# Attention and ELU-MLP in one kernel: transposed scores in the first batch, one queue of eight PSUM banks, and a sort key for each step

## The chip, the cores and the metric

The kernel runs on one NeuronCore of a Trainium2 chip. TensorE (PE) does the matmuls, VectorE (DVE), ScalarE (ACT) and GpSimd (POOL) the rest; SyncE (SP) issues the DMAs. The metric is device time in microseconds. The kernel before takes 1371.11 us, the median of three runs (1369.72 to 1373.3).

## The reference

```
q_n = q / sqrt(mean(q*q) + 1e-6) * g_q          (the same for k)
scores = q_n @ k_n.T / 8                        batch 8, heads 12, seq 448, head size 64
attn = exp(scores - max(scores));  attn /= sum(attn) + 1e-9
x = attn @ v, heads side by side                3584 tokens x 768
h = x @ w_in                                    768 x 2048
g = where(h > 0, h, exp(min(h, 0)) - 1)
out = g @ w_out                                 2048 x 768
```

## The kernel before

**Units of work.** Heads go in pairs: 48 pairs `p`, six to a batch. The queries of a pair are cut into seven tiles (`T = 7 p + j`, j = 0 to 6) of 128 rows by 448 keys. A float32 operand is split into a high and a low float16 part, so that scores are three matmuls of 448 columns (`s_mm`, L539). A tile's scores lie in one PSUM bank; DVE takes the row maximum (`s_max`, L546), ACT writes exp(score - max) and the row sum (`s_exp`, L560), POOL adds 1e-9 to the sum (`s_z`, L564), DVE inverts it (`s_rec`, L572).

**From the second batch on**, ACT writes the scaled high part into a float16 buffer (`s_hi`, L605; three such buffers, `p16`), DVE the low part (`s_lo`, L610), which frees the bank, and a transposing DMA on SP's queue (`s_tr`, L621) puts the tile into `ptall` with keys on the partitions. There is one such place for a pair, so a pair's transposes wait until the pair before has been multiplied with v: `attend`, L638, 22 matmuls, two at a time on two halves of the array. `x_high` and `x_low` (L645, L657) read that result.

**In the first batch** the weights are still being prepared, and the transposing is done by TensorE: POOL makes a diagonal matrix with the inverse sums (`s_diag`, L576), four float32 matmuls per tile transpose and scale (`s_pe`, L584), ACT copies the result to SBUF (`s_hi`, L601), and `attend` multiplies in float32.

**The MLP** of a batch is 576 matmuls of 448 columns: 288 for the first product (`mlp`, L733; 16 blocks `f` of 18) and 288 for the second (L747; six blocks of 48). It runs beside the attention of the following batch. Each first-product block leaves its bank in five steps (`m1_out`): exp on ACT (L670), a second ACT step (L674), the minimum and maximum on DVE (L678, frees the bank), the high part on ACT (L684), the low part on DVE (L687). A second-product block needs one ACT copy (L708). Below, a pair beside the first product is called an **M1 pair**, one beside the second an **M2 pair**: three and three to a batch.

**Weights.** `conv` splits each of 16 blocks of `w_in` and 24 of `w_out`: ACT L235 and L236, DVE L241 and L265, sums over partitions by `column_sums` (13 or 9 matmuls of 64 columns, L135), then L281/L284 or L306 to L321. Queries and keys are normalised by `qk_square` to `qk_transpose` (L363 to L430).

**Order.** Nothing is scheduled at run time; each engine takes its instructions in the order in which they are written. Time is a counter `h`, 14 units to a pair. The table `SCHED` gives each step an `h` in halves; a loop over `h` writes the steps due, then the MLP matmuls due by a rate (576 for 84 units), in two or three stretches around the score matmuls. For all pairs after the first batch a tile's steps have the same offsets (`tile`, second row), two units apart from tile to tile. Scores are issued for four tiles and then, eight units later, for three; `attend` of the pair before is written right behind those three. The bank queue is first in, first out: five banks, seven from the second batch on; `av` is a bank of its own.

Of the kernel before, what the change touches and what calls it, by code (L numbers as in the profile page):

```python
# [20 lines left out]
NPAIR = H // 2  # L21
# [11 lines left out]
def tile_attention_then_elu_mlp(ctx: ExitStack, tc: tile.TileContext, qk, v, v_scan, gg, w_in, w_out, out):  # L33
# [46 lines left out]
    nc.vector.memset(eps, 1e-6)  # L80

    def cols(t, n):
# [22 lines left out]
        t[:CK].rearrange("p (c q) -> p c q", c=4)  # L105
# [25 lines left out]
    def column_sums(parts, bank):  # L131


        for i, a in enumerate(parts + [tiny]):
            nc.tensor.matmul(bank[:, S:], ones, a, start=i == 0, stop=i == len(parts))  # L135

    def largest(bank, e):
        nc.vector.tensor_reduce(out=e, in_=bank[:, S:], axis=AX.X, op=ALU.max)
        return e
# [74 lines left out]
    def conv(src, i, width, acol, bank, parts):  # L216
# [7 lines left out]
        ws = None  # L224
# [21 lines left out]
        def s_sums():  # L246
            column_sums([upper(t[:, a : a + 64]) for a in range(0, width, 64)], bank)
# [22 lines left out]
        steps = [load, s_act, s_join, s_sign, on_pe(s_sums), s_scale]  # L270
        for fn in parts:
            step = lambda fn=fn: fn(w, ws)
            steps.append(on_pe(step) if fn in late else step)
        loads.add(load)
        return steps

    def conv_in(f):
# [5 lines left out]
        def s_low(w, ws):  # L283
# [6 lines left out]
            w_in, f, WI_W, a_in[:, f : f + 1], sb[4 - f] if f < 2 else av,  # L290
            [s_high, s_low],
        )

    def conv_out(i):
# [30 lines left out]
        def s_store(w, ws):  # L325
# [3 lines left out]
            w_out, i, WO_W, most[:, i : i + 1], mb[i % 2] if i < WO_OWN else av,  # L329
# [129 lines left out]
    def v_steps(b):  # L459

        m1 = dg = None
# [6 lines left out]
        def two():  # L468
            nonlocal dg
# [3 lines left out]
        def three():  # L473
            column_sums([upper(dg[:, :64]), upper(dg[:, 64:])], av)
# [544 lines left out]
```

## Time and profile before

| | |
|---|---|
| median of three runs | 1371.11 us |
| the profiled execution | 1372.15 us, span 1370.3 us |
| mean granted TensorE clock | 0.975 |
| busy in the span: PE, ACT, DVE, POOL | 91%, 64%, 61%, 36% |
| `attend` of pairs 5, 11, 47 starts at | 143.1, 321.2, 1254.6 us |

The span lies 1.85 us below the time of its own execution. Busy time counts recorded instructions, and neighbouring records on one engine overlap slightly, so that the step from start to start is a little shorter than a record. `[3.33 <-PE av L638]` behind a row means that the engine stood idle for 3.33 us and that this instruction ended the wait.

### The profile page before, as it was taken

The page shows a single profiled execution, that of the slowest core. Times are in us where ns is not written, and L with a number is a line of the kernel's source. Part 1 is how long each engine was busy: PE and PEld are TensorE (multiplying, and loading weights), DVE is VectorE, ACT ScalarE, POOL GpSimd, SP SyncE. Part 2 cuts the span into 40 slices and gives each one's busy share as a digit, 9 for nine tenths or more (in the row PEclk, how much of TensorE's full clock was granted, in tenths as well). Part 3 has the DMA queues.
Part 4 walks back from the last instruction along what each step waited for, and adds up shares of the span by engine and source line. Part 5 has one row for each costly group of instructions (what it writes and reads, how often), then busy time and mean ns, then how long its engine had stood idle before and what let it go on. Part 6 is the DMA issues. An engine that isn't in the chain of part 4 may idle for free.

```text
span 1370.3 us, 22209 instructions
## 1 busy us (share of the span) xinstructions
PE 1249.1 (91%) x7564; PEld 724.8 (53%) x7564; DVE 840.8 (61%) x1898; ACT 883.2 (64%) x1857; POOL 488.8 (36%) x823
## 2 busy tenths in 40 slices
PE   4898988989899988999889998999889988999998
PEld 2555444654446643565436644565446644466566
DVE  8998877776665656656665656655666556642310
ACT  7999787656676567756765567746766566743520
POOL 4677543444233422433323432333333333231000
PEclk9999899999999999999999999999999999999999
DMA  9557776886558866597556866588446965574011
GB/s 341 159 171 169 158 179 149 196 199 128 111 120 183 190 108 133 112 209 160 107 117 160 202 124 133 109 199 174 106 105 157 210 121 113 109 151 121 1 44 58
DMA packets 405713, 198.62 MB, mean 145 GB/s; under 512 B 367968, under 2 KB 381920, under 8 KB 405600
## 3 DMA queue, kind: packets, MB, share of 16 engines
q1 hardware_dynamic: 405600, 197.21, 63.6%
q8 instruction: 59, 0.97, 0.3%
q14 instruction: 54, 0.44, 0.1%
HBM read 93.52 MB, written 14.16 MB: 79 GB/s over the span
## 4 chain that ended last, share of the span: by engine, by line
PE 59%; ACT 16%; DVE 11%; DMA 7%; issue 6%; POOL 1%; SPq 0%; ACTq 0%; POOLq 0%; DVEq 0%
PE s L747 22%; PE s L733 10%; PE av L638 7%; PE m L747 6%; DMA ptall<-p 6%; PE s L539 5%; PE m L733 4%; ACT p L605 4%; DVE p L610 3%; ACT s L560 2%; PE m L539 2%; ACT gall L684 2%; DVE st L546 2%; PE s L584 2%; DVE e L678 2%
## 5 line engine op out<-in xcount | busy, mean ns | idle before, releaser
L747 PE MATMUL s<-gall,whos 128*128 128x448 f16 x1184 | 325.0, 354 | 0.1
L610 DVE SCALAR_TENSOR_TENSOR p<-s,st,p 128x448 f16<-128x448 f32 x204 | 139.5, 684 | 256.4 <-ACT p L605 255.0
L733 PE MATMUL s<-x,whi 128*128 128x448 f16 x1022 | 290.0, 364 | 4.3 <-DVE p L610 2.4
L564 POOL TENSOR_SCALAR st<-st 128x1 f32<-128x1 f32 x336 | 78.1, 232 | 589.0 <-ACT s L560 391.8
L747 PEld LDWEIGHTS <-whos 128*128 128x128 f16 x1536 | 221.2, 144 | 80.4 <-issue 13.8
L733 PEld LDWEIGHTS <-whi 128*128 128x128 f16 x1536 | 153.7, 100 | 160.9 <-issue 33.5
L747 PE MATMUL s<-gall,wls 128*128 128x448 f16 x592 | 209.8, 354 | 0.0
L539 PE MATMUL s<-qkt 64*128 64x448 f16 (+1 forms) x840 | 148.5, 369 | 52.6 <-DVE p L610 33.3
L560 ACT ACTIVATE s<-s,st 128x448 f32<-128x448 f32 x204 | 122.7, 602 | 109.5 <-DVE st L546 104.0
L733 PE MATMUL s<-x,wli 128*128 128x448 f16 x511 | 185.7, 363 | 0.0
L605 ACT ACTIVATE p<-s,st 128x448 f16<-128x448 f32 x204 | 127.9, 627 | 60.1 <-DMA ptall<-p 59.0
L546 DVE TENSOR_REDUCE st<-s 128x1 f32<-128x448 f32 x246 | 151.4, 615 | 9.8 <-PE s L539 8.3
L539 PEld LDWEIGHTS <-qkt 64*128 64x128 f16 (+1 forms) x1152 | 55.4, 98 | 173.2 <-issue 141.8
L747 PEld LDWEIGHTS <-wls 128*128 128x128 f16 x768 | 111.3, 145 | 40.3 <-issue 7.7
L610 DVE SCALAR_TENSOR_TENSOR p<-m,st,p 128x448 f16<-128x448 f32 x90 | 61.5, 683 | 112.0 <-ACT p L605 111.5
L392 POOL TENSOR_TENSOR nat<-nat,r 128x896 f32<-128x896 f32 (+1 forms) x48 | 84.7, 1766 | 109.9 <-DVE r L382 108.7
L684 ACT ACTIVATE gall<-e,gsc 128x448 f16<-128x448 f32 x128 | 85.1, 665 | 59.3 <-DVE e L678 59.1
L733 PEld LDWEIGHTS <-wli 128*128 128x128 f16 x768 | 76.8, 100 | 79.2 <-issue 17.0
L687 DVE SCALAR_TENSOR_TENSOR gall<-e,gsc,gall 128x448 f16<-128x448 f32 x128 | 98.2, 767 | 23.3 <-ACT gall L684 22.6
L733 PE MATMUL m<-x,whi 128*128 128x448 f16 x354 | 99.7, 361 | 1.9 <-DVE p L610 1.9
L747 PE MATMUL m<-gall,whos 128*128 128x448 f16 x352 | 98.8, 361 | 1.8 <-DVE p L610 1.8
L674 ACT ACTIVATE e<-e,nisc,isc 128x448 f32<-128x448 f32 x128 | 96.6, 754 | 1.2
(129 smaller groups left out, 1992.0 us busy)
## 6 DMA issues: line engine op xcount, KB each, us to landing
wls<-wl_d SPq DMA_DIRECT2D x48, 512.0 KB, 4.0
nat<-in_qk SPq DMA_DIRECT2D x48, 448.0 KB, 3.9
raws<-in_w_out SPq DMA_DIRECT2D x24, 512.0 KB, 4.7
out<-y SPq DMA_DIRECT2D x48, 224.0 KB, 2.6
vn<-in_v SPq DMA_DIRECT2D x38, 256.0 KB, 3.3
vscan<-in_v_scan SPq DMA_DIRECT2D x36, 224.0 KB, 3.7
whos<-in_w_in SPq DMA_DIRECT2D x10, 768.0 KB, 6.7
ptall<-p SPq DMA_TRANSPOSE x336, 3.1
```

What stands on the lines that cost most here:

```text
L392: nc.gpsimd.tensor_tensor(out=n[:, a:], in0=n[:, a:], in1=r[:, a:], op=ALU.mult)
L539: nc.tensor.matmul(ps[r0 : r0 + n, :S], qq[rows, a, q0 : q0 + n], qq[rows, z, S:], start=(a + z == 0), stop=(a == 1),)
L546: nc.vector.tensor_reduce(out=st[:, 0:1], in_=pss[T][:, :S], axis=AX.X, op=ALU.max, negate=True)
L560: nc.scalar.activation(e, ps, AF.Exp, bias=st[:, 0:1], accum_out=st[:, 1:2])
L605: nc.scalar.activation(p16[:, :S], pss[T][:, :S], AF.Copy, scale=stats[T][:, 2:3])
L610: nc.vector.scalar_tensor_tensor(out=p16[:, S:], in0=ps[:, :S], scalar=r, in1=p16[:, :S], op0=ALU.mult, op1=ALU.subtract)
L638: nc.tensor.matmul(av[64 * h : 64 * h + 64, :S], vs[:, h], ps[h], start=(k == 0), stop=(k == len(terms) - 1),)
L674: nc.scalar.activation(e, e, AF.Identity, scale=isc, bias=nisc)
L684: nc.scalar.activation(g[:, 0], e, AF.Copy, scale=gsc)
L687: nc.vector.scalar_tensor_tensor(out=g[:, 1], in0=e, scalar=gsc, in1=g[:, 0], op0=ALU.mult, op1=ALU.subtract)
L733: nc.tensor.matmul(ph[:, :S], w[:, c, :], x[:, r, :], start=(c == 0 and i == 0), stop=last)
L747: nc.tensor.matmul(py[:, :S], w, g[:, r, :], start=(f == 0 and i == 0), stop=last)
```

## The change

**First batch.** Scores are computed twice. The first time (`s_mm`, two tiles at a time) they serve only for the maximum: `s_max` writes the negated maxima of all seven tiles into one small array and gives the bank back. POOL splits the maxima into two bfloat16 parts (`m_last`, `m_split`). The second time (`t_mm`) they are computed with keys on the partitions, in seven banks per pair; `t_shift` adds the negated maxima to the same banks, with 64 matmuls a pair of 128 columns (or 64), the maxima broadcast as weights and an identity as the moving operand. `t_exp` is then one ACT instruction per tile straight into the buffer that `attend` reads. The sums over keys are eight float32 matmuls with ones (`t_sum`); the inverse is exp(-ln z) on ACT with one Newton step on DVE (`z_log`, `z_inv`, `z_newton`, `x_times`, `x_step`), applied to the result of `attend`. `s_diag`, `s_pe`, and the first batch's `s_exp`, `s_z`, `s_rec` and `s_hi` are gone.

**Banks.** All eight are in one queue; `attend`, `column_sums` and the score tiles take from it.

**Order.** Every step has its own key with three decimals; a heap takes the steps in the order of their keys. The MLP is placed matmul by matmul, with a pace for the first two batches and the old rate afterwards; the offsets of `m1_out` and `m2_out` are a table (`evict`). Pairs from 12 on share one pattern of keys, repeated every 14 units.

```diff
+    banks = [psum.tile([128, S], F32, name=f"b{i}") for i in range(8)]
...
     def s_max(T):
+        p, j = divmod(T, NJ)
+        if by_pe(T):
+            to = mneg[p % 2][:, 8:] if j == NJ - 1 else mneg[p % 2][:, j % 2 * 4 + j // 2 :][:, :1]
+        else:
+            st = stats[T] = small("st", 3, bufs=6)
+            to = st[:, 0:1]
+        nc.vector.tensor_reduce(out=to, in_=pss[T], axis=AX.X, op=ALU.max, negate=True)
+        if by_pe(T):
+            give(pss.pop(T))
...
+    def t_mm(p, c):
+        qq = qkt[p].rearrange("p t j n -> p t (j n)")
+        k0 = S + 128 * c
+        if c < 3:
+            pst[p, c] = [take(), take()]
+        else:
+            ps = take()
+            pst[p, c] = [ps[:64], ps[64:], ps]
+        for a, z in ((0, 0), (0, 1), (1, 0)):
+            for h in (0, 1):
+                rows = slice(64 * h, 64 * h + 64)
+                nc.tensor.matmul(
+                    pst[p, c][h], qq[rows, a, k0 : min(k0 + 128, 2 * S)], qq[rows, z, :S],
+                    start=(a + z == 0), stop=False,
+                )
+
+    def t_shift(p, c):
+        m = mhl[p % 2].rearrange("p t (h i) -> p t h i", h=2)
+        for i in range(4):
+            for t in (0, 1):
+                for h, ps in enumerate(pst[p, c][:2]):
+                    nc.tensor.matmul(
+                        ps[:, 128 * i : min(128 * i + 128, S)],
+                        m[:, t, h, i : i + 1].broadcast_to([128, ps.shape[0]]),
+                        eye if i < 3 else eye2, start=False, stop=(i == 3 and t == 1),
+                    )
+
+    def t_exp(p, j):
+        c, h = divmod(j, 2)
+        ps = pst[p, c][h] if c < 3 else pst[p, c][2]
+        nc.scalar.activation(pt_f32[p % 2][:, j], ps, AF.Exp)
+        give(ps)
...
+        av = avs[p] = take()
...
+    def next_mm(i, key):
+        r = next(moe, None)
+        if r:
+            for d, fn in zip(SCHED["evict"][2 * (i >= 576) + (len(r) == 3)], r, strict=True):
+                at(key + d, fn)
+        if i + 1 < 576 * B:
+            key = pace(i + 1)
+            at(key, next_mm, i + 1, key)
...
-        [-0.5, 0.5, 1.5, 1.5, 2.5, 3, 6, 8.5, 4.5],
+        [169.723, 170.697, 171.11, 172.729, 173.518, 173.963, 177.243],
```

The three places below lie in the fourth batch, beside the first product of the third, where the pattern of the later batches is in force.

TensorE at `attend` of pair 18 and the last three score tiles of pair 19; `vt` is the v of the pair, `qkt` its queries and keys, `s4`, `b3` and the like are banks. Before:

```order
L539 MATMUL s4_71<-qkt_5136 128x448
L539 LDWEIGHTS qkt_5136
L539 MATMUL s2_69<-qkt_5136 128x448
...
L539 MATMUL s3_70<-qkt_5136 64x448
L638 LDWEIGHTS vt_5478
L638 MATMUL av_72<-ptall_135,vt_5478 64x448
...
L733 LDWEIGHTS wli5_114
L733 MATMUL m0_73<-x3_129,wli5_114 128x448
```

And now:

```order
L788 LDWEIGHTS whi5_114
L788 MATMUL b1_68<-x3_145,whi5_114 128x448
...
L689 LDWEIGHTS vt_5660
L689 MATMUL b3_70<-ptall_151,vt_5660 64x448
...
L533 LDWEIGHTS qkt_5373
L533 MATMUL b7_74<-qkt_5373 128x448
L533 LDWEIGHTS qkt_5373
L533 MATMUL b5_72<-qkt_5373 128x448
```

`attend` stood behind three score tiles, each of which waits for a free bank; it now stands ahead of them and takes one bank itself.

ScalarE between `x_high` of pairs 18 and 19 (L560 is `s_exp`, L605 `s_hi`, L670, L674 and L684 the steps of `m1_out`, L401 and L411 copies of keys and queries). Before:

```order
L560 ACTIVATE s4_71,st_5589<-s4_71,st_5589 128x448
L605 ACTIVATE p16_5611<-m1_74,st_5523 128x448
L674 ACTIVATE e_5602<-e_5602,nisc_2177,isc_2176 128x448
L401 ACTIVATE t16_5632<-nat_5316 128x384
L670 ACTIVATE e_5635<-m0_73,sc_2175 128x448
L560 ACTIVATE s2_69,st_5626<-s2_69,st_5626 128x448
L605 ACTIVATE p16_5645<-s4_71,st_5589 128x448
L411 ACTIVATE t16_5632<-nat_5316 128x512
L684 ACTIVATE gall_134<-e_5602,gsc_2178 128x448
L674 ACTIVATE e_5635<-e_5635,nisc_2177,isc_2176 128x448
L560 ACTIVATE s3_70,st_5665<-s3_70,st_5665 128x448
L605 ACTIVATE p16_5680<-s2_69,st_5626 128x448
```

And now (L639 is `s_exp`, L655 `s_hi`, L725, L729 and L739 the steps of `m1_out`, L398 the copy of the keys):

```order
L739 ACTIVATE gall_150<-e_5790,gsc_3591 128x448
L639 ACTIVATE b4_71,st_5802<-b4_71,st_5802 128x448
L655 ACTIVATE p16_5831<-b0_67,st_5664 128x448
L725 ACTIVATE e_5835<-b1_68,sc_3588 128x448
L729 ACTIVATE e_5835<-e_5835,nisc_3590,isc_3589 128x448
L739 ACTIVATE gall_150<-e_5835,gsc_3591 128x448
L725 ACTIVATE e_5864<-b3_70,sc_3588 128x448
L398 ACTIVATE t16_5867<-nat_5420 128x384
L729 ACTIVATE e_5864<-e_5864,nisc_3590,isc_3589 128x448
L655 ACTIVATE p16_5872<-b7_74,st_5776 128x448
L655 ACTIVATE p16_5881<-b5_72,st_5769 128x448
L655 ACTIVATE p16_5891<-b4_71,st_5802 128x448
```

An `s_exp` and the `s_hi` of the tile before it stood next to each other all through the pair; now the exponentials and the high parts come in groups, with whole MLP evictions between them.

VectorE in the same stretch (L610 is `s_lo`, L546 `s_max`, L572 `s_rec`, L678 and L687 steps of `m1_out`, L367 a sum for the next pair). Before:

```order
L610 SCALAR_TENSOR_TENSOR p16_5645<-s4_71,st_5589,p16_5645 128x448
L546 TENSOR_REDUCE st_5665<-s3_70 128x1
L572 RECIPROCAL st_5626<-st_5626 128x1
L687 SCALAR_TENSOR_TENSOR gall_134<-e_5602,gsc_2178,gall_134 128x448
L678 SCALAR_TENSOR_TENSOR e_5635<-e_5635,m0_73 128x448
L610 SCALAR_TENSOR_TENSOR p16_5680<-s2_69,st_5626,p16_5680 128x448
L546 TENSOR_REDUCE st_5709<-s1_68 128x1
```

And now (L651 is `s_rec`, L660 `s_lo`, L733 and L742 steps of `m1_out`, L545 `s_max`, L364 the sum):

```order
L660 SCALAR_TENSOR_TENSOR p16_5872<-b7_74,st_5776,p16_5872 128x448
L733 SCALAR_TENSOR_TENSOR e_5864<-e_5864,b3_70 128x448
L660 SCALAR_TENSOR_TENSOR p16_5881<-b5_72,st_5769,p16_5881 128x448
L742 SCALAR_TENSOR_TENSOR gall_150<-e_5835,gsc_3591,gall_150 128x448
L660 SCALAR_TENSOR_TENSOR p16_5891<-b4_71,st_5802,p16_5891 128x448
L545 TENSOR_REDUCE st_5918<-b7_74 128x1
L545 TENSOR_REDUCE st_5922<-b3_70 128x1
L364 TENSOR_REDUCE ss_5929<-qkt_5911 128x14
L545 TENSOR_REDUCE st_5937<-b0_67 128x1
```

Each maximum stood right behind the `s_lo` of an earlier tile; now the maxima stand together, ahead of or behind a group of `s_lo`.

## Rows read from the trace of the kernel before

**Rows 1.** The page: span, busy time of the engines, and the granted clock in 40 slices of the span, in tenths.
```profile
span 1370.3 us, 22209 instructions
PE 1249.1 (91%) x7564; PEld 724.8 (53%) x7564; DVE 840.8 (61%) x1898; ACT 883.2 (64%) x1857; POOL 488.8 (36%) x823
PEclk9999899999999999999999999999999999999999
```
**Rows 2.** Busy time by stretch: the first batch up to `attend` of pair 5, the second up to that of pair 11, the next six, and what is left after the last `attend`. Columns: stretch, length, busy time of PE, PEld (weight loads), DVE, ACT and POOL with instructions, granted clock, DMA share, GB/s.
```profile
0.00:143.50 143.50, 112.66 (x874) 70.10 (x876) 128.40 (x298) 126.81 (x257) 91.22 (x132) 0.98 0.70 213
143.50:321.16 177.66, 155.99 (x987) 87.27 (x985) 131.62 (x297) 127.67 (x267) 81.92 (x119) 0.94 0.76 170
321.16:1254.62 933.46, 868.37 (x5107) 496.24 (x5109) 559.36 (x1271) 592.11 (x1278) 314.34 (x567) 0.98 0.67 142
1254.62:1370.30 115.68, 112.07 (x603) 71.21 (x602) 21.45 (x34) 36.65 (x56) 1.34 (x5) 1.00 0.13 42
```
**Rows 3.** The same view of the six stretches of three M1 pairs, from one `attend` to the third after it: the first and the second of them and the sum of the six.
```profile
321.16:405.79 84.63, 75.07 (x430) 35.64 (x432) 52.88 (x115) 59.37 (x124) 26.30 (x45) 0.96 0.56 116
475.71:563.26 87.55, 75.56 (x432) 35.65 (x433) 53.59 (x116) 60.42 (x128) 26.64 (x46) 0.96 0.58 114
...
sum 516.60, PE 451.90 PEld 214.16 DVE 321.19 ACT 361.09 POOL 159.47; mean PE 75.32 PEld 35.69 DVE 53.53 ACT 60.18 POOL 26.58
```
**Rows 4.** The same view of the first stretch of three M2 pairs, and of one M1 pair alone.
```profile
405.79:475.71 69.92, 69.91 (x428) 47.16 (x430) 41.81 (x101) 39.61 (x90) 26.96 (x50) 1.00 0.82 182
506.41:534.64 28.23, 24.25 (x145) 11.66 (x146) 16.90 (x38) 19.64 (x41) 8.55 (x15) 1.00 0.51 109
```
**Rows 5.** Waits over the whole span: who waited for whom, total us, times, longest.
```profile
PE s L539 <- DVE p L610: 33.3, 25, 2.7
DVE p L610 <- ACT p L605: 366.5, 259, 4.7
ACT p L605 <- DMA ptall<-p: 87.3, 55, 4.3
```
**Rows 6.** Groups of instructions in the three M1 pairs from 475.71 to 563.26 us: busy time, mean ns of one, idle time before them and what ended it.
```profile
L610 DVE SCALAR_TENSOR_TENSOR p<-s,st,p 128x448 f16<-128x448 f32 x16 | 10.9, 684 | 21.7 <-ACT p L605 21.4
L610 DVE SCALAR_TENSOR_TENSOR p<-m,st,p 128x448 f16<-128x448 f32 x5 | 3.4, 684 | 8.9 <-ACT p L605 8.9
L684 ACT ACTIVATE gall<-e,gsc 128x448 f16<-128x448 f32 x14 | 9.3, 666 | 8.7 <-DVE e L678 8.7
L687 DVE SCALAR_TENSOR_TENSOR gall<-e,gsc,gall 128x448 f16<-128x448 f32 x13 | 10.4, 799 | 0.1
```
**Rows 7.** The timeline of one M1 pair (start us, duration us, what, wait before it), ACT, DVE and SP's queue.
```profile
511.71 0.63 ACT L605 ACTIVATE p<-m,st 128x448 f16<-128x448 f32 x1 [0.81 <-DMA ptall<-p]
512.25 0.75 ACT L674 ACTIVATE e<-e,nisc,isc 128x448 f32<-128x448 f32 x1
512.38 0.68 DVE L610 SCALAR_TENSOR_TENSOR p<-m,st,p 128x448 f16<-128x448 f32 x1 [2.52 <-ACT p L605]
512.90 0.51 ACT L401 ACTIVATE t<-nat 128x384 f16<-128x384 f32 x1
512.98 0.67 DVE L687 SCALAR_TENSOR_TENSOR gall<-e,gsc,gall 128x448 f16<-128x448 f32 x1
513.57 0.62 DVE L546 TENSOR_REDUCE st<-s 128x1 f32<-128x448 f32 x1
514.23 0.61 ACT L560 ACTIVATE s<-s,st 128x448 f32<-128x448 f32 x1 [0.29 <-DVE st L546]
514.85 0.63 ACT L605 ACTIVATE p<-s,st 128x448 f16<-128x448 f32 x1
...
516.22 1.23 SPq L621 DMA_TRANSPOSE ptall<-p  x1
```
**Rows 8.** The first batch: TensorE's timeline, matmuls merged.
```profile
84.07 0.74 PE L539 MATMUL s<-qkt 64*128 64x448 f16 x3
84.74 1.13 PE L584 MATMUL s<-dgz,ex 128*112 128x128 f32 x8
85.70 0.52 PE L135 MATMUL av<-wts,ones 128*128 128x64 bf16 x12
86.06 0.19 PE L135 MATMUL av<-tiny,ones 128*128 128x64 bf16 x1
87.91 3.23 PE L638 MATMUL av<-ptall,gall 112*64 112x448 f32 x16
93.18 0.76 PE L539 MATMUL s<-qkt 64*64 64x448 f16 x6
```
**Rows 9.** Groups of the first 250 us: what the change takes out of the first batch, and `x_low`, whose form the new DVE steps have.
```profile
L560 ACT ACTIVATE ex<-s,st 128x448 f32<-128x448 f32 x42 | 26.5, 632 | 4.1 <-DVE st L572 1.2 <-PE s L584 1.1 <-PE av L135 0.8
L560 ACT ACTIVATION_READ_ACCUMULATOR ex<-s,st 128x1 f32 x42 | 8.5, 202 | 0.0
L601 ACT ACTIVATE ptall<-s 112x512 f32<-112x512 f32 x21 | 12.6, 601 | 0.0
L576 POOL TENSOR_SCALAR dgz<-ident,st 128x128 f32<-128x128 f32 x42 | 23.0, 547 | 7.2 <-DVE st L572 2.0 <-DVE most L138 1.5 <-PE s L584 0.4
L572 DVE RECIPROCAL st<-st 128x1 f32<-128x1 f32 x69 | 10.5, 153 | 1.2 <-POOL st L564 1.2
L652 DVE SCALAR_TENSOR_TENSOR x<-av,vs,x 128x448 f16<-128x448 f32 x6 | 4.0, 671 | 0.0
```

More of the change, by code (lines that the diff above doesn't have):

```diff
@@ L129, in upper, with column_sums @@
         return t.bitcast(BF16).rearrange("p (n w) -> p n w", w=2)[:, :, 1]
-    def column_sums(parts, bank):
-        for i, a in enumerate(parts + [tiny]):
-            nc.tensor.matmul(bank[:, S:], ones, a, start=i == 0, stop=i == len(parts))
+    def column_sums(pairs):
+        bank = take()
+        pairs = pairs + [(ones, tiny)]
+        for i, (w, a) in enumerate(pairs):
+            nc.tensor.matmul(bank[:, :64], w, a, start=i == 0, stop=i == len(pairs) - 1)
+        return bank
     def largest(bank, e):
-        nc.vector.tensor_reduce(out=e, in_=bank[:, S:], axis=AX.X, op=ALU.max)
+        nc.vector.tensor_reduce(out=e, in_=bank[:, :64], axis=AX.X, op=ALU.max)
+        give(bank)
         return e
@@ L246, in s_sums @@
         def s_sums():
-            column_sums([upper(t[:, a : a + 64]) for a in range(0, width, 64)], bank)
+            nonlocal bank
+            bank = column_sums([(ones, upper(t[:, a : a + 64])) for a in range(0, width, 64)])
         def s_scale():
@@ L268, in s_sign @@
             )
[L270 to L275, printed above, removed]
+        steps = [load, s_act, s_join, s_sign, s_sums, s_scale]
+        return steps + [lambda fn=fn: fn(w, ws) for fn in parts]
     def conv_in(f):
@@ L459, in v_steps @@
     def v_steps(b):
-        m1 = dg = None
+        m1 = bank = None
         def one():
@@ new lines, in tile_attention_then_elu_mlp, with t_sum, z_log @@
+    avs, zbs, zes, zas = {}, {}, {}, {}
+    def t_sum(p):
+        zb = zbs[p] = take()
+        pt = pt_f32[p % 2]
+        for c in range(4):
+            for h in (0, 1):
+                nc.tensor.matmul(
+                    zb[64 * h : 64 * h + 64], one3[:, 0 if c < 3 else 1 + h], pt[:, min(2 * c + h, 6)],
+                    start=c == 0, stop=c == 3,
+                )
+    def z_log(p):
+        zes[p] = pool.tile([128, S], F32, tag="e", name="ze", bufs=3)
+        nc.scalar.activation(zes[p], zbs[p], AF.Ln, bias=small9)
@@ new lines, in z_inv, with z_newton, x_times, x_step @@
+    def z_inv(p):
+        nc.scalar.activation(zes[p], zes[p], AF.Exp, scale=-1.0)
+    def z_newton(p):
+        zas[p] = pool.tile([128, S], F32, tag="e", name="za", bufs=3)
+        zb = zbs.pop(p)
+        nc.vector.scalar_tensor_tensor(
+            out=zas[p], in0=zb, scalar=1e-9, in1=zes[p], op0=ALU.add, op1=ALU.mult
+        )
+        give(zb)
+    def x_times(p):
+        av = avs.pop(p)
+        nc.vector.tensor_tensor(out=zes[p], in0=av, in1=zes[p], op=ALU.mult)
+        give(av)
+    def x_step(p):
+        nc.vector.scalar_tensor_tensor(
+            out=zas[p], in0=zas[p], scalar=2.0, in1=zes.pop(p), op0=ALU.subtract, op1=ALU.mult
+        )
```

380 lines of the change are left out of this document (189 added, 191 removed), and 118 rows, old and new, of the table SCHED.

## The prediction

> **What bounds the kernel now.** I read the page first, then busy time by stretch, then the waits, then one pair's timeline. The page says that PE is busy for 91% of the span [rows 1], so most of the time is TensorE's own work; what the change can win is PE's idle time, and where that lies the stretches tell [rows 2]: 30.8 us of 143.5 in the first batch, 21.7 us in the second, 65.1 us in the six that follow, 3.6 us at the end. After the last `attend` both kernels have the same 580 MLP matmuls left, so what counts is when that `attend` comes.
>
> In the six later batches the two kinds of pair differ. Three M2 pairs take 69.92 us with PE busy for 69.91, which is 23.3 us a pair and TensorE alone [rows 4]. Three M1 pairs take 516.6 / 6 = 86.1 us, 28.7 us a pair, though PE issues the same number of matmuls, while ACT is busy for 20.1 us of it and DVE for 17.8 [rows 3]. So no engine is full: 5.4 us a pair are lost to waiting, 18 pairs, 97 us. The clock explains little: one M1 pair at a granted clock of 1.00, the 2.4 GHz level, still takes 28.2 us [rows 4].
>
> The waits give the reason. PE waits for banks that DVE's L610 has not yet freed, 33.3 us under one set of bank names alone; DVE's L610 waits for ACT's L605, 366.5 us in 259 waits; ACT's L605 waits for transposing DMAs to free a float16 buffer, 87.3 us [rows 5]. In three M1 pairs DVE stands 30.3 us in front of L610, 1.4 us for each of 21 tiles, and ACT stands 8.7 us in front of L684 because the DVE step before it is queued behind that L610 [rows 6]. The timeline shows the circle: high part at 511.71, low part at 512.38, an MLP step, the next maximum at 513.57, its exponential at 514.23, the next high part at 514.85 [rows 7]. That is 3.1 us a tile, seven times 22 us, in which ACT and DVE hand over to one another four times a tile; what else ACT has to wait for in a pair (the transposing, `x_high`) comes on top.
>
> **The change part by part, M1 pairs.** The work of each engine in these pairs stays as it was: same steps, same sizes. Order and banks change. `attend` moves ahead of three score tiles, so it waits for one bank instead of three, and the transposing that follows it starts earlier. Exponentials and high parts come in groups of one to three tiles, and no maximum stands any more directly behind a low part that waits for ACT. I followed ACT and DVE by hand through one M1 pair in the new order, with start-to-start steps from the timeline (0.62 us for an exponential, 0.54 for a high part, 0.65 for the MLP's second step) [rows 7]. ACT then has these waits left: 0.7 us for the end of `attend`, 1.0 us for the first maximum behind it, 0.6 and 0.4 us for MLP steps behind maxima on DVE, 0.3 us for the transposing. That is 3.0 us on 20.1 us of work, 23.1 us, about what PE needs by itself. The walk is too smooth in two places. DVE's L687 takes 0.80 us on average where the walk has 0.67 [rows 6, 7], 0.7 us for 5.3 blocks. And it lets every transposing land at its usual time, though the longest wait for one is 4.3 us [rows 5]; I add 1.0 us. That makes 25.0 us a pair. The bounds are 23.3 us, PE alone, and 28.7 us, as before; I take a value nearer to the lower one because the circle that sets 28.7 is taken apart, but not PE's own value, because ACT has hardly more room than the waits listed. 18 pairs at 28.7 - 25.0 = 3.7 us: **67 us less**. The M2 pairs are PE's own work: 0.
>
> Behind `attend`, now earlier, TensorE's queue holds the score tiles; in front of SP's transposes stand the same loads as before. In the second pattern the last three high parts stand together on ACT, and each waits for a buffer that an earlier tile's transposing frees; SP needs 1.23 us to issue one [rows 7]. Queued behind them are the next block's MLP steps, for whose bank PE waits.
>
> **First batch.** Per pair, ACT loses seven exponentials with their read of the sum (0.63 + 0.20 us recorded) and seven copies of 0.60, and gains seven exponentials without a sum and two more passes of that size, nine at 0.63: 10.0 - 5.7, 4.3 us less [rows 9]. DVE loses seven reciprocals of 0.15 us and gains three steps of the form of `x_low`, 0.67 each: 1.0 us more [rows 9]; without the overlap of short records it is nearer to 1.3, 8 us for six pairs with the constants. POOL loses seven diagonal matrices of 0.55 us and the scaling of the sums, 23.0 us and more in the batch [rows 9], against four small copies and subtractions a pair.
>
> TensorE: one tile's scores alone take 0.67 us from start to start, two half-height ones side by side no longer (0.76 recorded), and a tile's transposing 0.96 to 1.1 us [rows 8]: 7 x (0.67 + 1.05) = 12.0 us go. Scores of two tiles side by side, twice, are eight times 0.67 = 5.4 us; `t_sum` has the form of the first batch's `attend`, 3.2 us [rows 8]; `t_shift` has no row. Twelve matmuls of 64 columns start within 0.36 us, 0.03 each [rows 8], and matmuls of 448 columns every 0.22, three to a tile's 0.67; between them 128 columns come to 0.06, 64 of them to 3.8 us a pair. Bounds: 0.03 and 0.22 each, 1.9 to 14 us. I take the value between the two, since the form differs only in the number of columns. Sum 12.4 us against 12.0: nothing. The Trainium skill (TensorE: Matmul & The Clock Gate, Back-to-back issue gap) puts a stream of weight load and 128-column matmul at about 81 ns a matmul; by that `t_shift` would be an estimated 5.2 us a pair, and no run here shows it. It would add 1.4 us a pair to PE, which has 30.8 us free in this batch [rows 2], so the sum below would stay.
>
> DVE and ACT are both nearly full in the first batch, 128.4 and 126.8 of 143.5 us [rows 2]. Relief on ACT and POOL therefore wins little while DVE gets 8 us more; part of that fits into its 15 us of idle time. And one wait is new: no exponential of a pair can run before all its seven maxima. I take **4 us more**, between -5 (ACT's relief closes a third of DVE's idle time) and +12 (8 plus a chain that shows in part).
>
> **Second batch.** Six pairs take 177.7 us, 29.6 each, with PE busy for 156.0 [rows 2]; the same handing over is at work, beside the weights' conversion. Bounds 0 and 21.7 us less; I take **10 us less**, under half, since DVE and ACT still do the conversion.
>
> **Sum.** 1372.15, the profiled execution, + 4 - 10 - 67 = 1299 us. That execution lies 1 us above the median of the three, which puts the median of the changed kernel at 1298; I say 1299.
>
> **Rivals.**
> *A. TensorE becomes the bound of M1 pairs as of M2 pairs.* For it: ACT's 20.1 and DVE's 17.8 us fit into 23.3 [rows 3, 4]. Against it: the waits in the walk. 97 us in the M1 pairs, 22 in the second batch, 5 in the first: 1371 - 124 = 1247 us.
> *B. The waits only change places.* ACT and DVE still cross for each MLP block and each tile; if the groups make one long wait of several short ones, M1 pairs come to 27.5 us. 18 x 1.2 = 22 us less, 4 more in the first batch: 1353 us. If the new keys make no difference in effect to what waits for what, no change is left.
> *C. Slower: the last high parts of a pair wait for transposes.* Three of them stand together on ACT, and MLP steps and their banks behind them. For it: 87.3 us already go in 55 such waits, up to 4.3 us [rows 5]. Against it: `attend` is earlier, and the third needs only the fourth tile's transposing. It decides from 5.4 us of waiting a pair, at which an M1 pair is back at 28.7. At 6 us a pair takes 29.3: 18 x 0.6 = 11 more, 4 in the second batch's pairs, 8 in the first: 1371 + 23 = 1394 us.
>
> **How the numbers follow.** Forecast 0.43, with a range of its own from 1275 to 1330; A 0.20; B 0.21, a quarter of it within 0.3% of before; C 0.16. About 0.3% is what a measurement of this kernel can tell from no change, 1367 to 1375 us. Faster 0.43 + 0.20 + 0.16 = 0.79, same 0.05, slower 0.16. From 1252 to 1376 us: A's lower part (0.08) and C's upper one (0.12) are left out.
>
> **What would show it.** Right: three M1 pairs between two `attend`s at 73 to 78 us; DVE's idle time before the low part under 12 us in three M1 pairs, where it was 30.3; `attend` of pair 5 at 140 to 155 us; about 0.06 us for a matmul of `t_shift`. Wrong: M1 pairs above 27 us with ACT idle before the high parts on transposes (C) or before exponentials on maxima (B); M1 pairs at 23.3 us with PE never idle (A); a first batch beyond 155 us, where the chain from the seventh maximum to the first exponential is longer than I allow.

## The result, and the profile after

The changed kernel takes 1273.31 us (median of 4 runs, 1269.55 to 1274.1) against 1370.49 us for the kernel before on the same chip: 0.928 of it, 95% interval 0.926 to 0.931, or 97 us less. The forecast was 1299 us, 26 us too slow. The measured time lies inside the stated bounds of 1252 to 1376 us, but outside the range of 1275 to 1330 that the forecast had for itself; it is as far from rival A's 1247 us as from the 1299.

The page after: span, busy time of the engines, granted clock in 40 slices, and the chain that ended last.

```profile
span 1271.1 us, 22591 instructions
PE 1215.2 (96%) x7852; PEld 704.2 (55%) x7852; DVE 863.7 (68%) x1883; ACT 860.1 (68%) x1777; POOL 481.1 (38%) x763
PEclk9889899999999999999999999999999999999999
PE 68%; DVE 4%; ACT 2%; issue 1%; POOL 0%; DMA 0%; ACTq 0%; POOLq 0%
```

TensorE is busy for 96% of the span where it was 91% [rows 1]. Busy time by the same four stretches as in [rows 2] (columns as there):

```profile
0.00:151.07 151.07, 116.01 (x1148) 57.35 (x1148) 142.04 (x273) 102.02 (x176) 61.73 (x71) 0.92 0.63 190
151.07:318.85 167.78, 152.40 (x1010) 87.15 (x1009) 139.53 (x298) 128.79 (x269) 87.05 (x119) 0.99 0.83 186
318.85:1155.42 836.57, 834.78 (x5100) 488.33 (x5100) 561.82 (x1279) 591.33 (x1278) 331.04 (x569) 1.00 0.78 160
1155.42:1271.10 115.68, 112.07 (x602) 71.32 (x602) 20.33 (x34) 37.97 (x56) 1.33 (x5) 1.00 0.13 42
```

Against [rows 2] the first batch is 7.6 us longer, the second 9.9 shorter, the six that follow 96.9 shorter, the tail the same: 99.2 us together, the difference of the two spans. In the third stretch PE stands idle for 1.8 us of 836.6, where it stood for 65.1 of 933.5.

The stretches of three M1 pairs, the second and third of six and the sum, as in [rows 3]:

```profile
457.25:527.13 69.88, 69.83 (x426) 34.50 (x426) 52.76 (x118) 57.57 (x119) 27.47 (x43) 1.00 0.77 144
596.90:667.01 70.11, 70.05 (x430) 34.34 (x429) 52.89 (x118) 57.90 (x119) 27.46 (x43) 1.00 0.70 140
...
sum 418.93, PE 417.14 PEld 204.85 DVE 319.62 ACT 347.90 POOL 166.68; mean PE 69.52 PEld 34.14 DVE 53.27 ACT 57.98 POOL 27.78
```

418.93 us instead of 516.60: 97.7 us, so all of the third stretch's gain lies in the 18 M1 pairs, now at 23.3 us like the M2 pairs [rows 4]. Two numbers make it up. PE's idle time falls from 516.60 - 451.90 = 64.7 us to 1.8. And its busy time falls by 34.8 us, from 451.90 to 417.14, for the same work. The granted clock goes from 0.96 [rows 3] (0.96 in the other four stretches too) to 1.00: 0.04 of 516.60 us, some 21 of the 34.8, are matmuls that no longer run at the 1.2 GHz level. What the other 14 are is taken up below the table of runs.

The waits after, those that answer to [rows 5]:

```profile
DVE p L660 <- ACT p L655: 122.6, 101, 4.0
ACT p L655 <- DMA ptall<-p: 66.6, 50, 3.6
PE b L533 <- DVE p L660: 2.4, 3, 1.1
```

The low part's wait for the high part is a third of what it was, PE's wait for the low part's bank is nearly gone, and ACT's wait for the transposing has only shrunk by a quarter. In one stretch of three M1 pairs (457.25 to 527.13 us), the groups that answer to [rows 6]:

```profile
L660 DVE SCALAR_TENSOR_TENSOR p<-b,st,p 128x448 f16<-128x448 f32 x19 | 12.7, 675 | 4.8 <-ACT p L655 4.8
L655 ACT ACTIVATE p<-b,st 128x448 f16<-128x448 f32 x20 | 12.1, 625 | 2.9 <-DMA ptall<-p 1.4 <-DVE st L651 1.1 <-DVE p L660 0.3
L742 DVE SCALAR_TENSOR_TENSOR gall<-e,gsc,gall 128x448 f16<-128x448 f32 x13 | 11.6, 891 | 0.0
L739 ACT ACTIVATE gall<-e,gsc 128x448 f16<-128x448 f32 x14 | 9.3, 665 | 5.3 <-DVE e L733 4.3 <-DVE gsc L493 0.8
```

DVE stands 4.8 us in front of the low parts where it stood 30.6 [rows 6]. ACT still waits 5.3 us in front of the MLP's fourth step, and nothing comes of it: that time now lies beside PE's.

### The profile page after: what moved, and what is told of

It is laid out like the page before. It is cut to its first block, busy times and chain, and to the rows that moved or that the text cites. A ratio compares the mean times of both kernels' runs of the same rounds, so it can differ in the third digit from the quotient of the medians.

```text
span 1271.1 us, 22591 instructions
## 1 busy us (share of the span) xinstructions
PE 1215.2 (96%) x7852; PEld 704.2 (55%) x7852; DVE 863.7 (68%) x1883; ACT 860.1 (68%) x1777; POOL 481.1 (38%) x763
## 4 chain that ended last, share of the span: by engine, by line
PE 68%; DVE 4%; ACT 2%; issue 1%; POOL 0%; DMA 0%; ACTq 0%; POOLq 0%
PE b L802 30%; PE b L788 25%; PE b L533 7%; PE b L689 6%; DVE gall L742 1%; DVE st L545 1%; ACT p L655 1%; DVE p L660 1%; ACT b L639 1%; ACT e L725 0%; DVE e L733 0%; DMA ptall<-p 0%; ACT e L729 0%; ACT gall L739 0%; DVE ss L375 0%
## 5 line engine op out<-in xcount | busy, mean ns | idle before, releaser
L802 PE MATMUL b<-gall,whos 128*128 128x448 f16 x1536 | 417.3, 353 | 2.5 <-DVE gall L742 2.5
L788 PE MATMUL b<-x,whi 128*128 128x448 f16 x1376 | 376.8, 354 | 1.9 <-DVE e L733 1.1
L660 DVE SCALAR_TENSOR_TENSOR p<-b,st,p 128x448 f16<-128x448 f32 x294 | 196.6, 676 | 124.9 <-ACT p L655 122.6
L802 PE MATMUL b<-gall,wls 128*128 128x448 f16 x768 | 272.8, 355 | 0.0
L788 PE MATMUL b<-x,wli 128*128 128x448 f16 x688 | 243.7, 354 | 0.0
L655 ACT ACTIVATE p<-b,st 128x448 f16<-128x448 f32 x294 | 179.8, 628 | 94.2 <-DMA ptall<-p 66.6
L545 DVE TENSOR_REDUCE st<-b 128x1 f32<-128x448 f32 x294 | 173.0, 615 | 89.6 <-PE b L533 89.5
L639 ACT ACTIVATE b<-b,st 128x448 f32<-128x448 f32 x294 | 177.2, 603 | 41.4 <-DVE st L545 38.5
L533 PE MATMUL b<-qkt 64*128 64x448 f16 (+1 forms) x1152 | 142.9, 359 | 14.6 <-DVE mneg L545 8.9
L733 DVE SCALAR_TENSOR_TENSOR e<-e,b 128x448 f32<-128x448 f32 x128 | 79.0, 617 | 92.0 <-ACT e L729 91.7
L739 ACT ACTIVATE gall<-e,gsc 128x448 f16<-128x448 f32 x128 | 85.2, 666 | 45.2 <-DVE e L733 38.9
L742 DVE SCALAR_TENSOR_TENSOR gall<-e,gsc,gall 128x448 f16<-128x448 f32 x128 | 109.2, 853 | 0.2
L689 PE MATMUL b<-ptall,vt 128*64 128x448 f16 x924 | 96.5, 355 | 3.1 <-POOL vt L452 2.9
L729 ACT ACTIVATE e<-e,nisc,isc 128x448 f32<-128x448 f32 x128 | 97.2, 760 | 2.2
L389 POOL TENSOR_TENSOR nat<-nat,r 128x896 f32<-128x896 f32 (+1 forms) x48 | 82.3, 1715 | 39.6 <-DVE r L379 23.3
```

The lines of the kernel that those rows point to most:

```text
L389: nc.gpsimd.tensor_tensor(out=n[:, a:], in0=n[:, a:], in1=r[:, a:], op=ALU.mult)
L533: nc.tensor.matmul(ps[r0 : r0 + n], qq[rows, a, q0 : q0 + n], qq[rows, z, S:], start=(a + z == 0), stop=(a == 1),)
L545: nc.vector.tensor_reduce(out=to, in_=pss[T], axis=AX.X, op=ALU.max, negate=True)
L639: nc.scalar.activation(ps, ps, AF.Exp, bias=st[:, 0:1], accum_out=st[:, 1:2])
L655: nc.scalar.activation(p16[:, :S], pss[T], AF.Copy, scale=stats[T][:, 2:3])
L660: nc.vector.scalar_tensor_tensor(out=p16[:, S:], in0=ps, scalar=r, in1=p16[:, :S], op0=ALU.mult, op1=ALU.subtract)
```

## The experiments

Each kernel is timed against the kernel before on the same chip (medians of before: 1372.4 to 1373.9 us beside the experiments). The measure below is the stretch from `attend` of pair 17 to that of pair 47 beside the whole time: thirty pairs, in which PE alone needs some 697 us. Each trace gives it. A trace is one execution: it lies within 1.7 us of the median in the table, but the one of "before, both" took 1331.96 us, 7 more than its median.

| kernel | time, us | pairs 17 to 47, us | PE busy in them, us |
|---|---|---|---|
| before | 1370.5 | 778.9 | 723.4 |
| before, `attend` early | 1339.6 | 753.5 | 717.4 |
| before, eight banks | 1356.9 | 762.6 | 714.6 |
| before, both | 1325.1 | 744.8 | 713.6 |
| both, and MLP steps closer | 1319.9 | 736.5 | 709.1 |
| both, and earlier tile first | 1310.0 | 729.9 | 710.9 |
| changed | 1273.3 | 698.1 | 697.8 |
| changed, `attend` late | 1289.7 | 712.2 | 698.9 |
| changed, old tiles, `attend` late | 1318.3 | 721.9 | 704.4 |
| changed, old tiles, `attend` early | 1286.4 | 696.2 | 695.2 |
| the same, MLP on the old grid | 1288.1 | 699.8 | 696.9 |
| the same, old places of v maxima and scales | 1292.0 | 699.4 | 696.0 |

Of the 80.8 us between the first row and the changed kernel, 55.2 are PE's idle time and 25.6 its busy time. The windows of before, of the changed kernel, and of the one with old tiles and late `attend` (columns as in [rows 2]) tell how much of the latter is the clock:

```profile
475.64:1254.55 778.91, 723.39 (x4253) 413.44 (x4251) 464.68 (x1055) 493.20 (x1066) 261.08 (x473) 0.98 0.67 142
457.25:1155.35 698.10, 697.83 (x4261) 407.96 (x4260) 463.93 (x1060) 490.90 (x1057) 272.71 (x471) 1.00 0.78 159
477.30:1199.23 721.93, 704.42 (x4249) 411.38 (x4247) 473.11 (x1059) 488.26 (x1060) 273.39 (x472) 1.00 0.74 153
```

A mean granted clock of 0.98 over 778.91 us is worth about 16 of the 25.6 us. The rest is not the clock: with old tiles and late `attend`, PE stands idle for 17.5 us at a granted clock of 1.00, and its busy time is 6.6 us above that of the changed kernel all the same. A matmul's record (0.35 us) is longer than the step to the next matmul (0.22 us, [rows 8]), so that each stop begins under a record that counts as busy; whether that is all of the rest was not measured.

### `attend` ahead of the score tiles

In the changed kernel, one number puts it behind again:

```diff
-        [169.199, 169.18, 175.358, 175.386, 189.341],
+        [169.199, 169.18, 175.358, 175.386, 189.387],
```

> The changed kernel with attend of a steady pair issued behind the three score tiles of the next pair again instead of ahead of them (one number of the table); everything else as changed (1273 us, three M1 pairs about 70 us). Theory G (the grouping of exponentials and high parts broke the circle between ACT and DVE): at most 1285 us, three M1 pairs 70 to 73 us. Theory H (attend ahead of the score tiles is what shortens the pair): 1320 to 1350 us, three M1 pairs 78 to 84 us, PE waiting in front of the score tiles. Theory Q (eight banks in one queue with the MLP's new places): 1273 us within 5.

1289.67 us, ratio to before 0.940 (0.938 to 0.941). Sixteen us of the changed kernel's gain go, 14 of them in pairs 17 to 47, where an M1 pair takes 23.7 to 25.7 us. That is between G and H: `attend`'s place counts, but in the new order it is worth 14 us and not 60.

In the kernel before, the same move the other way:

```diff
-            mm = [lambda mm=mm: (*(fn() for fn in mm), attend(p - 1))]
+            mm = [lambda mm=mm: (attend(p - 1), *(fn() for fn in mm))]
```

> The kernel before with one edit: attend of the pair before is issued ahead of the last three score tiles. Theory G: 1360 to 1371 us, M1 pairs at 28 us or more. Theory H: 1290 to 1320 us, three M1 pairs 72 to 77 us. Theory Q: 1371 us within 5.

1339.61 us, 0.975 (0.972 to 0.978): 31 us, 25 of them in pairs 17 to 47. Below G's number, above H's: a real part, not the whole. The first two M1 pairs of a batch come to 24 to 27 us, the third stays at 30 to 32.

### The pattern of the score tiles

```diff
+            if p >= 12:
+                last = {0: 8.5, 6: 4.5}
+                rows = [
+                    [168 + 2 * j + d for d in (-0.5, 0.5, 1.5, 1.5, 2.5, 3, last.get(j, 6))]
+                    for j in range(NJ)
+                ]
...
-        [169.199, 169.18, 175.358, 175.386, 189.341],
+        [167.25, 167.25, 175.25, 175.25, 189.3],
```

> The changed kernel with the old pattern of the score tiles from pair 12 on: each tile's maximum, exponential, sums, high and low part at the old distances from one another, score tiles in fours and threes, attend behind them; the queue of eight banks, the MLP's new places and the first two batches stay. Theories G and H: 1345 to 1370 us, three M1 pairs 83 to 87 us, DVE idle before the low part near 30 us in three M1 pairs. Theory Q: under 1290 us, three M1 pairs under 73 us.

1318.29 us, 0.961 (0.958 to 0.963), M1 pairs 23.9 to 25.3 us. No theory has this number: it is too fast for G and H and too slow for Q. Against the changed kernel with late `attend` (1289.7 us), 9.7 of the 28.6 us lie in pairs 17 to 47 and most of the others between pairs 9 and 17. With 189.2 for the last number, `attend` stands ahead:

> As the run with the old pattern of the score tiles, but attend of the pair before stands ahead of the last three score tiles. Theory G: 1340 to 1365 us, hardly less than with attend behind. Theory H: 1280 to 1300 us. Theory Q: as the run with the old pattern, under 1290 us.

1286.44 us, 0.937 (0.935 to 0.939). This was a surprise: from pair 17 on this kernel is as fast as the changed one, 696.2 us, every M1 pair but one at 23.1 to 23.3. Its 13 us are lost before: between pairs 9 and 17 it takes 208.3 us against 189.9, and earlier and later pairs give some of that back. So the new grouping in ones to threes is not needed in the steady part, if `attend` is early; G falls there in the form in which it was stated, and H holds only together with something that the kernel before with early `attend` lacks.

### What does the kernel before still lack?

The eighth bank, alone and with early `attend` (`attend` takes a bank of the queue and `x_low` gives it back):

```diff
-                    av[64 * h : 64 * h + 64, :S], vs[:, h], ps[h], start=(k == 0),
+                    avs[p][64 * h : 64 * h + 64, :S], vs[:, h], ps[h], start=(k == 0),
...
+        avs[p] = av if p < 12 else take()
...
+        if p > 10:
+            give(avs[p])
```

> The kernel before with attend's own bank put into the queue as the eighth from pair 12 on (attend takes one, x_low gives it back; the v scale's sums take one too). What is left between the kernel before and the changed kernel with old tiles and late attend (1318 us) is the question. Theory Q (the eighth bank): 1315 to 1335 us. Theory V (the MLP's steps after an accumulation follow one another closely, so its bank comes back sooner): 1365 to 1371 us. Theory K (neither: the places of the other steps): 1365 to 1371 us.

> The kernel before with both edits, attend ahead of the last three score tiles and the eighth bank in the queue. Theory Q: 1285 to 1305 us, three M1 pairs 70 to 73 us. Theories V and K: 1330 to 1340 us, as with the early attend alone (1340 us).

1356.92 us, 0.990 (0.987 to 0.992), and 1325.05 us, 0.967 (0.964 to 0.969). The bank is worth 15 us either way, much less than Q asks, and more than the nothing of V and K: both times lie between the theories' numbers. Where the time still goes, windows of the second of these kernels show: the second and the third M1 pair of a batch, and two parts of the latter (columns as in [rows 2]):

```profile
643.24:666.87 23.63, 23.52 (x143) 11.36 (x142) 16.02 (x35) 17.73 (x38) 7.44 (x13) 1.00 0.67 133
666.87:698.94 32.07, 27.08 (x143) 12.40 (x142) 21.70 (x45) 23.05 (x49) 10.14 (x17) 0.89 0.55 110
...
675.00:683.00 8.00, 6.18 (x35) 2.92 (x34) 4.97 (x9) 5.10 (x11) 1.93 (x3) 1.00 0.97 201
683.00:691.00 8.00, 6.31 (x22) 2.37 (x21) 5.47 (x13) 6.72 (x13) 2.15 (x5) 0.63 0.30 57
```

The second M1 pair takes 23.6 us, the third 32.1 with the same 143 matmuls; 4.9 us of its surplus are idle time, and 3.6 are busy time, most of which the granted clock of 0.63 from 683 to 691 us accounts for. TensorE's timeline shows what it did before that (matmuls that waited):

```profile
682.75 0.35 PE L543 MATMUL s<-qkt 64*128 64x448 f16 x1 [1.82 <-DVE p L614]
683.87 0.35 PE L543 MATMUL m<-qkt 64*128 64x448 f16 x1 [0.78 <-DVE e L687]
...
686.95 0.90 PE L742 MATMUL s<-x,whi 128*128 128x448 f16 x2 [0.91 <-DVE p L614]
```

It stood 1.82 and 0.78 us, for banks that a low part and an MLP step had not yet given back; behind that the granted clock fell to the 1.2 GHz level, and PE stopped for another 0.91 us. ACT and DVE at that place:

```profile
680.75 0.58 ACT L564 ACTIVATE s<-s,st 128x448 f32<-128x448 f32 x1
...
681.35 0.62 ACT L609 ACTIVATE p<-s,st 128x448 f16<-128x448 f32 x1
```

```profile
682.01 0.68 DVE L614 SCALAR_TENSOR_TENSOR p<-s,st,p 128x448 f16<-128x448 f32 x1 [1.33 <-ACT p L609]
```

The exponential of one tile (680.75) stands ahead of the high part of the tile before it (681.35), and DVE's low part waits for that high part. This is the circle of [rows 7], still there.

The MLP's steps closer together, in that kernel:

```diff
-                    steps_at(h + 1, enumerate(r))
+                    steps_at(h + 1, zip((0, 0.5, 1, 1.5, 4) if done > 1152 and len(r) == 5 else range(5), r))
```

> As the kernel before with both edits, and the MLP's first four steps after an accumulation of M1 placed 0.5 apart from the second group of six pairs on, where they stood 1 apart, so that its bank is given back one place sooner. Theory Q: as the run without this edit, within 5 us. Theory V: 1285 to 1305 us where the run without it has about 1335. Theory K: 1325 us or more in both.

1319.94 us, 0.961 (0.959 to 0.963). (One of the 128 blocks, the seventh of the last batch, loses two ACT steps of its five here, at the end of the main loop.) Five us by the medians, eight in pairs 17 to 47: V does not hold, K's 1325 us or more is missed as well, and Q has already fallen. From the other side, the kernel with old tiles and early `attend` and the MLP's matmuls and steps on the old grid:

```diff
-                at(key + d, fn)
+                at(key + d if i < 1152 or len(r) == 3 else int(key) + [1, 2, 3, 4, 5][r.index(fn)], fn)
...
             key = pace(i + 1)
+            key = key if i < 1152 else int(key) + 0.25
```

> The changed kernel with the old pattern of the score tiles, attend ahead of the last three (1286 us so far), and from the third batch on the MLP back on the old grid: all matmuls of a half step together, and the five steps behind an accumulation of M1 one whole place apart, 1 to 5. The kernel before with early attend and eight banks takes 1325 us; the 39 us between them are the question. Theory M (the places of the MLP's steps): 1315 to 1330 us, with PE idle and a lower granted clock in the third M1 pair. Theory O (the places of the other steps: q and k, v, the maxima of v, the MLP's scales): 1284 to 1290 us, M1 pairs at 23.3.

1288.14 us, 0.938 (0.935 to 0.941): M falls; the MLP's places alone do next to nothing (3.6 us in pairs 17 to 47). And the old places of v's maxima and the MLP's scales (two rows of the table, scan and m, with the numbers of before):

> The changed kernel with the old pattern of the score tiles and early attend (1286 us so far), and with the old places of two kinds of steps from the second batch's end on: the loads, maxima and scale of the next v, and the eight small steps of the MLP's scales. In the kernels before, the third M1 pair is the slow one (28 to 32 us with early attend and eight banks). Theory O: 1300 to 1320 us, the third M1 pair at 26 us or more. Theory M: 1286 us within 4, all M1 pairs at 23.2 to 23.5.

1292.04 us, 0.940 (0.937 to 0.943). Neither number, but the M1 pairs are M's: pairs 17 to 47 take 699.4 us, every third M1 pair 23.2. Of the 5.6 us by which this kernel is slower, some four are lost in the second batch and three in pairs 17 to 47. These steps are not it either.

A look at the order on ACT gave the next theory. My "old pattern" was not the old one: where a tile's high part and the next tile's exponential fall on the same half step, the kernel before enters the tiles in falling order, so the exponential comes first; my edit entered them in rising order, so the high part came first. One more edit puts that one thing into the kernel before with early `attend` and eight banks:

```diff
-    for T in reversed(range(NCHUNK)):
+    for T in [*range(12 * NJ, NCHUNK), *reversed(range(12 * NJ))]:
```

> The kernel before with early attend and eight banks (1325 us), and one thing more: from pair 12 on the tiles are entered in rising order, so that where steps of two tiles fall on the same half step the earlier tile's comes first. On ACT the high part of a tile then stands ahead of the next tile's exponential instead of behind it, on DVE the reciprocal ahead of the next maximum; places of q, k, v, MLP, matmuls and DMAs stay as in the kernel before. The runs with the old pattern had entered the tiles in rising order, unlike the kernel before. Theory G2 (this order is the rest of the circle: a low part waits for a high part that stands behind another tile's exponential): 1280 to 1297 us, M1 pairs at 23.3 to 24. Theory O2 (the new places of the q, k and v steps are the rest): 1318 to 1330 us, the third M1 pair at 27 us or more.

1310.03 us, 0.953 (0.949 to 0.957): 15 us less by the medians. The two traces lie 20.6 us apart, since that of the kernel without this edit lies 7 us above its median; 14.9 of these lie in pairs 17 to 47. Neither number: the order is a part, about a third of what was left, and the third M1 pairs stay at 27 to 28 us. One of them (window, then ACT and SP's queue):

```profile
659.62:687.67 28.05, 25.47 (x143) 11.98 (x142) 20.08 (x42) 21.40 (x46) 11.26 (x17) 0.94 0.60 119
```

```profile
668.98 0.63 ACT L609 ACTIVATE p<-av,st 128x448 f16<-128x448 f32 x1 [3.49 <-DMA ptall<-p]
```

```profile
663.63 0.57 SPq L342 DMA_DIRECT2D nat<-in_qk  x1
664.31 4.88 SPq L625 DMA_TRANSPOSE ptall<-p  x3
```

Here ACT stands 3.49 us for a buffer whose transposing is late; three transposes stand on SP's queue behind the load of q and k and take 4.88 us. PE then idles 2.5 us and runs part of the pair at the lower clock (0.94 over the pair). That this load or another step of q, k and v is to blame was read, not tried: its old places were not run in the changed kernel. So some 32 us of pairs 17 to 47 (729.9 to 698.1) stay open, between the places of the q, k and v steps and several places acting together.

### The first batch

The gain of q for pairs 1 to 6 on DVE instead of POOL:

```diff
-        eng = nc.gpsimd if 0 < p <= NPAIR else nc.vector
-        eng.tensor_tensor(
+        nc.vector.tensor_tensor(
```

> The changed kernel with the gain of q for pairs 1 to 6 (a multiplication of two SBUF operands, 128 x 512) on DVE instead of POOL. Theory L (in the first batch DVE's steps with two SBUF operands stand still while POOL runs one of its own, 1.0 to 1.5 us each time, as the trace of the changed kernel shows at 19.3, 31.3 and 75.3 us): attend of pair 5 at 144 to 149 us instead of 151, the time 1266 to 1272 us. Theory W (DVE is full with its own work, and 0.68 us more a pair makes it later): attend of pair 5 at 153 to 156 us, the time 1275 to 1279 us.

1277.2 us, 0.930 (0.929 to 0.932), `attend` of pair 5 at 156.28 us.

```profile
0.00:156.28 156.28, 114.89 (x1147) 57.97 (x1148) 142.25 (x274) 102.63 (x175) 49.20 (x62) 0.93 0.60 183
```

The time is W's, the busy time is L's: DVE took over six steps of 0.68 us and is busy for 142.25 us as before the move (142.04), so its other steps became some 4 us shorter in sum, with less of POOL's work beside them. But DVE's idle time grew from 9.0 to 14.0 us, and the batch with it. DVE's sum alone does not set the batch.

The correction of the reciprocals left out:

```diff
-        nc.vector.scalar_tensor_tensor(
-            out=zas[p], in0=zb, scalar=1e-9, in1=zes[p], op0=ALU.add, op1=ALU.mult
-        )
...
-        nc.vector.scalar_tensor_tensor(
-            out=zas[p], in0=zas[p], scalar=2.0, in1=zes.pop(p), op0=ALU.subtract, op1=ALU.mult
-        )
+        zas[p] = zes.pop(p)
```

> The changed kernel without the two DVE steps that correct the reciprocal of the first batch's sums (z_newton and x_step; the correction and its sign are left out of the first batch's output). They take 0.62 and 0.81 us in the trace, six of each, 8.6 us. Theory W (DVE is the full engine of the first batch): attend of pair 5 at 142 to 146 us instead of 151, the time 1264 to 1269 us. Theory C (the chain from the seventh maximum to the exponentials and sums sets the batch): attend of pair 5 at 149 to 151 us, the time 1271 to 1275 us.

1266.29 us, 0.923 (0.919 to 0.926), `attend` of pair 5 at 147.89 us: 7 us in the whole time, as W has it, but only 3 of them by pair 5, between both theories. (Executions of one and the same first batch, in the runs that change only later parts, put that `attend` between 149.4 and 151.1 us.) DVE is nearly full and the chain matters too; which of them decides, these two runs do not settle.

## Why the prediction was right, and where it was off

**The M1 pairs.** The direction and the place were right: the gain lies in the M1 pairs, where ACT and DVE handed over to one another for each tile, and DVE's wait before the low part fell as forecast. The runs show three parts of it, which overlap: `attend` ahead of the score tiles (25 us of 81 in pairs 17 to 47 of the kernel before, 14 in the changed one), the eighth bank (16 alone, 9 behind the first, by the trace that lies 7 us above its median), and the order of high part and exponential (15 behind both). Together they are 49 of the 81 us; what the other 32 are stays open. And the changed kernel does not have the third part in that form: it writes up to three exponentials ahead of their high parts, and reaches the same 23.3 us.

The size was off: 25.0 us a pair was forecast, 23.3 measured, 18 pairs x 1.7 = 31 us, more than the error of the whole, since the first batch gave 4 us back. M1 pairs at 23.3 us with PE never idle were a sign against the forecast by its own list, and they are what came. Two steps failed.

- "ACT then has these waits left ... 23.1 us", then 0.7 for L687 and 1.0 for late transposing on top. The sum takes ACT's work and ACT's waits as the length of a pair. In the changed kernel ACT is busy for 347.90 / 18 = 19.3 us a pair (not for the 20.1 of before, which the prediction kept: by the sums of the stretches, 12 to 13 us of its work moved into the M2 pairs) and idle for 4.0, while PE stands idle for 1.8 us in all 18 pairs. So ACT's waits lay beside matmuls that PE had to run anyway, and PE alone set the pair. Of the two additions, L687's is there (L742 now, 891 ns), the transposing's is not: in the three pairs shown, L655 waits 1.4 us for it, 0.5 a pair, where the walk and the addition had 1.3.
- "The clock explains little." That rested on one pair at 1.00 [rows 4]. Over 18 pairs the granted clock was 0.96, about 21 of the 98 us. A walk through ACT and DVE cannot show this part. Nor does it follow from idle time alone, as the third window below the table of runs shows.

**The M2 pairs.** 0 forecast; 836.57 - 418.93 = 417.6 us against 933.46 - 516.60 = 416.9. Right.

**The second batch.** 10 us less forecast, 9.9 measured.

**The first batch.** 4 us more forecast, 7.6 measured, inside the bounds, with other terms than I gave. DVE's new steps are 15 for 10.3 us by the end of the stretch, against 6.4 us of reciprocals that are gone: 3.9 net, where I had 8. What I did not have is that DVE's old steps became longer. The joining and the sign of the weights' conversion, the same 26 steps, in the first batch of the changed kernel and of the kernel before:

```profile
L242 DVE SCALAR_TENSOR_TENSOR wts<-wts,w32s 128x768 uint32<-128x768 uint32 x16 | 18.8, 1176 | 0.3 <-ACT w32s L237 0.3
L267 DVE SCALAR_TENSOR_TENSOR w32s<-whos,wts 128x768 uint32<-128x768 uint32 x10 | 13.5, 1353 | 0.1
```

```profile
L241 DVE SCALAR_TENSOR_TENSOR wts<-wts,w32s 128x768 uint32<-128x768 uint32 x16 | 16.4, 1028 | 0.0
L265 DVE SCALAR_TENSOR_TENSOR w32s<-whos,wts 128x768 uint32<-128x768 uint32 x10 | 9.7, 969 | 0.0
```

That is 32.3 against 26.1 us. The section on the hardware has the reason.

**TensorE in the first batch.** 0.06 us was forecast for a 128-column matmul of `t_shift`. Its timeline, from one group of 32 to the group that follows:

```profile
115.70 1.75 PE L588 MATMUL b<-eye,mhl 128*128 128x128 bf16 x32
117.38 0.74 PE L578 MATMUL b<-qkt 64*128 64x448 f16 x6
```

The row's form is that of its first matmul; by forms the 32 are

```profile
L588 PE MATMUL b<-eye,mhl x32: 192/219/229, 115.7 to 117.2; 128*128 128x128 bf16 x24, 128*128 128x64 bf16 x8
```

In the trace the 24 of 128 columns start 0.056 us apart and the eight of 64 columns 0.029, at a granted clock of 1.00. So the forecast price was right; a pair has 48 and 16 of them, 3.2 us where 3.8 was forecast, which had all 64 at the full width. The Trainium skill's 81 ns (TensorE: Matmul & The Clock Gate, Back-to-back issue gap) does not hold for this stream; the measurement decides.

**The rivals.** A named the right state of the M1 pairs (23.3 us, PE never idle) and was 26 us too fast in all, because it closed the idle time of the first two batches as well. B and C did not come: the low parts wait a third of what they did, and the three high parts that stand together cost PE nothing.

## What to carry to other kernels

When two engines hand over to one another for each tile, look for whose bank or buffer the bound engine waits, and give those steps the front place on their queues: what reads the finished tile goes ahead of what starts the next. Read the granted clock behind TensorE's stops as well as the stops: here the lower clock cost 16 us beside 55 us of idle time in thirty pairs of one kernel, and nothing beside 17.5 us in another. Add a helper's wait to the time only where it delays the bound engine. When an order is rewritten for an experiment, compare the order that comes out, ties included, before blaming what is left.

## What the hardware did that was not expected

In these traces DVE's steps with two operands in SBUF stand still when they begin while POOL runs such a step. In the changed kernel's first batch, DVE and POOL:

```profile
31.25 2.45 DVE L267 SCALAR_TENSOR_TENSOR w32s<-whos,wts 128x768 uint32<-128x768 uint32 x1
33.62 2.02 DVE L282 SCALAR_TENSOR_TENSOR wli<-w32s,ws,whi 128x768 f16<-128x768 f32 x1
35.57 0.94 DVE L242 SCALAR_TENSOR_TENSOR wts<-wts,w32s 128x768 uint32<-128x768 uint32 x1
```

```profile
30.50 2.39 POOL L389 TENSOR_TENSOR nat<-nat,r 128x896 f32<-128x896 f32 x1 [0.65 <-DVE r L379]
32.97 1.86 POOL L403 TENSOR_TENSOR nat<-nat,gst 128x512 f32<-128x512 f32 x1
```

The first DVE step begins 0.75 us into a POOL step and takes 2.45 us, the second begins 0.65 us into the next one and takes 2.02; the third, alone, takes 0.94. Of the 26 steps counted above, six take 2.02 to 2.45 us in the changed kernel, and each of them begins inside a `tensor_tensor` of POOL; the other 20 take 0.94 to 0.96. In the kernel before only one of the 26 takes more than 1.2 us. The new places put such pairs side by side more often, which is the 6.2 us above. DVE's new steps that take one operand from a bank keep to 617 and 622 ns on average, the one with both in SBUF (`x_step`) takes 814. The Trainium skill states this (SBUF — State Buffer, Who interferes with whom): a DVE step with two SBUF inputs and a POOL step that reads SBUF exclude each other, and whichever begins later waits. The trace agrees.

And the granted clock fell behind short stops: in the kernel before with early `attend` and eight banks, PE stopped for 1.82 us (until 682.75) and for 0.78 us (until 683.87), and from 683 to 691 us the granted clock is 0.63, with PE busy for 6.31 of these 8 us. Not every kernel that stops shows this: with old tiles and late `attend`, PE stands idle for 17.5 us in thirty pairs at a granted clock of 1.00.
